# Two heads blocks on one core: where phi's VectorE part stands in the queue, one early transfer, one staging buffer

## The chip, the cores and the metric

The kernel runs on one core of one Trainium2 chip. The metric is the device time of one execution in microseconds (us). A core has five engines that matter here: TensorE (PE in the profile, with its weight loads shown as PEld), VectorE (DVE), ScalarE (ACT), GpSimd (POOL) and SyncE (SP, which issues most of the DMAs). Each engine takes its own instructions strictly in the order in which the program gives them to it, and engines wait for each other through semaphores.

## The reference

Two independent attention blocks run on inputs of 2048 tokens by 640 features, with 32 heads of 20 features, and their outputs are put side by side.

```
# A: attention over a sliding window of 256 keys
q, k, v = split(x @ wqkv)
scores  = q k^T * 20**-0.5, kept where 0 <= query - key < 256
o       = softmax(scores) @ v
a       = o @ wo

# B: linear attention, no softmax
phi(t)  = where(t > 0, t + 1, exp(t)) + 1e-6
kv, z   = sum_s phi(k) v^T, sum_s phi(k)
o       = (phi(q) @ kv) / (phi(q) @ z + 1e-6)
b       = o @ wo

out     = concatenate([a, b], axis=-1)        # bfloat16, 2048 x 1280
```

## The kernel before

All tokens are worked on in four blocks s = 0 to 3 of 512. The program is written out by hand in the order in which each engine is to take it; no scheduler moves anything.

**The score loop.** A's attention is cut into 90 score tiles (`units`, from `tiles_of`). For one tile `scores` lets TensorE write four heads' scores into `S_ps`, a tile of four PSUM banks of which there is one, lets ScalarE take the exponential of all of it into `p` (L582), and lets GpSimd zero what lies outside the window (`affine_select`, L596). Two tiles later (`LAG = 2`) `values` multiplies `p` with the values into `O_ps` (L618), one PSUM bank, of which there is one as well. When a group of heads is done, VectorE takes the reciprocal (`recA`, L640) and writes the normalised rows into `otokA` (L641). The next group's first matmul into `O_ps` has to wait for that.

**The filler.** Between two tiles, `take(credit)` draws matmuls from `fill`, a chain of Python generators with all other work: the projections of q, k and v of A (`a_qk`, `a_v`), the keys and values of B (`b_kv`), phi(q) of B (`b_q`), the denominators (`b_den`), the product of kv and wo (`b_merge`), and the output projections (`a_out`, `b_out`). A credit in matmul columns spreads it evenly over the 90 tiles. Each projection chain accumulates five matmuls into one `dense` PSUM bank (`bank`, `chain`, L201). There are three such banks, and the pool hands out the bank that was given back first in program order. Most banks are emptied by one VectorE copy (`evac`, L192).

**phi.** Where a bank holds B's q or k, `phi` empties it: ScalarE writes exp into a tile `e` (L210), VectorE clamps `e` in place (L214), and a second VectorE instruction (L217) reads the bank and `e` and writes phi. The two VectorE instructions are put off: they go into the list `later`, and `flush` issues them. In the kernel before, `flush` runs behind the next VectorE or ScalarE copy of another bank (`evac`) or behind the next exp (`phi`). For q, the put-off part also issues the DMA transpose `tok<-phi` on SP's queue (L498).

**Loads.** `spread(gen, loads, step)` issues x of a block as four DMA transposes on SP's queue (L689), one at every `step`-th matmul of `gen`. `("B", NS + 1)` stands for x of B's block 1, loaded a second time for `q[1]`, the second phi(q); it runs along with `q[0]`. On the same queue stand the transposes `oT<-otokA` (L652), `tok<-phi` (L498) and `wB<-wB` (L453, five for the merged weights).

**The tail.** After the last tile `a_out_last` projects A's last block, one row of 128 tokens at a time, through a staging buffer `osb` of a pool entry with two buffers, which the earlier output projections also use; their results leave by DMAs from GpSimd's queue (L384), the last ones from SP's (L673). `otokA` is another entry of that pool, also with two buffers.

Of the kernel before, what the change touches and what calls it, by code (L numbers as in the profile page):

```python
# [9 lines left out]
P = 128  # L10
# [3 lines left out]
BF16 = mybir.dt.bfloat16  # L14
# [7 lines left out]
TPS = SB // P  # L22
# [32 lines left out]
def kernel(  # L55
# [11 lines left out]
    _, S, D = A_x.shape  # L67
    KT = D // P
    NS = S // SB
# [7 lines left out]
    def pool(name, bufs, space=None):  # L77
        if space is None:
            return ctx.enter_context(tc.tile_pool(name=name, bufs=bufs))
        return ctx.enter_context(tc.tile_pool(name=name, bufs=bufs, space=space))  # L80
# [12 lines left out]
    op = pool("o", 2)  # L93
# [79 lines left out]


    later = []

    def flush():

        while later:
            later.pop(0)()  # L180

    both = []

    def evac(dst, src, to=None):

        if to is None and both:
            both.append(to)
            to = "AD"[len(both) % 2]
        if to == "A":
            nc.scalar.activation(out=dst, in_=src, func=ACT.Copy)  # L190
        else:
            nc.vector.tensor_copy(out=dst, in_=src)  # L192
        flush()

    def bank():
        return dps.tile([P, SB], F32, name="dense")

    def chain(dst, lhs, rhs, n):

        for kt in range(KT):  # L200
            nc.tensor.matmul(  # L201
                dst, lhsT=lhs(kt), rhs=rhs(kt), start=(kt == 0), stop=(kt == KT - 1)
            )
            if kt < KT - 1:
                yield n

    def phi(dst, src, view=lambda t: t[:], then=None):

        e = ep.tile([P, SB], BF16, name="e")
        nc.scalar.activation(out=view(e), in_=src, func=ACT.Exp)  # L210
        flush()

        def rest():
            nc.vector.tensor_scalar(  # L214
                out=e[:], in0=e[:], scalar1=1e-6, scalar2=1.0 + 1e-6, op0=ALU.add, op1=ALU.min
            )
            nc.vector.scalar_tensor_tensor(  # L217
                out=dst, in0=src, scalar=0.0, in1=view(e), op0=ALU.max, op1=ALU.add
            )
            if then is not None:  # L220
                then()

        later.append(rest)

    class End(int):
        pass
# [9 lines left out]
    def even(a, na, b, nb, lead=False):  # L236


        def one(g):
            for c in g:  # L240
                yield c
                if isinstance(c, End):
                    break

        done = 0
        for i in range(na):
            while lead and done < nb and done * na <= i * nb:
                done += 1
                yield from one(b)
            yield from one(a)  # L250
            while not lead and done * na < (i + 1) * nb:
                done += 1
                yield from one(b)
        yield from a
# [52 lines left out]
    def a_qk(s, between=()):  # L307
        yield from a_rows("q", s)
        for g in between:
            yield from g  # L310
        yield from drip(a_rows("k", s), ("q", s), 10, 4)
# [31 lines left out]
    def a_v(s):  # L343
        v_tok[s] = v_bufs[s % 3]
        yield from v_proj("A", xA[s], v_tok[s])
# [214 lines left out]
    def key(s, rel):  # L560
        return 4 * s + rel

    def scores(s, parts):
        S_ps = sps.tile([P, 4, SB], F32, name="S_ps")
        p_all = pp.tile([P, 4 * SB + 2], BF16, name="p")
        p = p_all[:, 0 : 4 * SB].rearrange("p (j q) -> p j q", j=4)
        nc.scalar.activation(out=p_all[0:1, 4 * SB : 4 * SB + 1], in_=ident[0:1, 0:1], func=ACT.Copy)  # L567
        for g, rel, blk, qs in parts:
            kb = key(s, rel)
            kt = k_pad[kb // TPS]  # L570
            ko = (kb % TPS) * P
            q0, n = qs[0][0] * P, len(qs) * P
            for j in range(4):
                nc.tensor.matmul(  # L574
                    S_ps[:, j, blk * P : blk * P + n],
                    lhsT=kt[32 * j : 32 * j + DH, g, ko : ko + P],
                    rhs=q_pad[s][32 * j : 32 * j + DH, g, q0 : q0 + n],
                    start=True,
                    stop=True,
                    tile_position=(32 * j, 0),  # L580
                )
        nc.scalar.activation(out=p, in_=S_ps[:], func=ACT.Exp, scale=scale)  # L582
        runs = []
        for _, _, blk, qs in sorted(parts, key=lambda x: x[2]):
            for i, (_, kind) in enumerate(qs):
                if kind == "F":
                    continue
                b = blk + i
                if runs and runs[-1][0] == kind and runs[-1][2] == b and b < runs[-1][1] + 2:
                    runs[-1][2] = b + 1  # L590
                else:
                    runs.append([kind, b, b + 1])
        for kind, b0, b1 in sorted(runs, key=lambda r: r[2] - r[1]):
            v = p[:, :, b0 * P : b1 * P].rearrange("p j (b q) -> p j b q", q=P)
            sgn = 1 if kind == "D" else -1
            nc.gpsimd.affine_select(  # L596
                out=v,
                in_=v,
                pattern=[[0, 4], [0, b1 - b0], [sgn, P]],
                compare_op=ALU.is_ge,  # L600
                fill=0.0,
                base=0 if kind == "D" else -1,
                channel_multiplier=-sgn,
            )
        return p
# [51 lines left out]
        yield from wo_proj(wo_sb["A"], 0, oT_A[s], s, 0)  # L657

    def a_out_last(s):
        osb = op.tile([P, TPS, D], BF16, name="osb")  # L660
        for tb in range(TPS):
            for lo, hi, to in ((0, SB, "A"), (SB, D, "D")):
                ps = bank()
                for _ in chain(
                    ps[:, 0 : hi - lo],
                    lambda kt: oT_A[s][:, kt, tb * P : (tb + 1) * P],
                    lambda kt: wo_sb["A"][:, kt, lo:hi],
                    hi - lo,
                ):
                    pass  # L670
                evac(osb[:, tb, lo:hi], ps[:, 0 : hi - lo], to)
            r0 = s * SB + tb * P
            nc.sync.dma_start(out=out2[r0 : r0 + P, 0:D], in_=osb[:, tb, :])  # L673
# [6 lines left out]
    def spread(gen, loads, step):  # L680

        parts = []
        for n, s in loads:
            def part(tb, n=n, s=s):
                x = xA if n == "A" else xB
                if tb == 0:
                    x[s] = xp.tile([P, KT, SB], BF16, name=f"x{n}")
                r0 = s % NS * SB + tb * P
                nc.sync.dma_start_transpose(  # L689
                    out=x[s][:, :, tb * P : (tb + 1) * P], in_=xsrc[n][r0 : r0 + P, :]  # L690
                )
            parts += [(part, tb) for tb in range(TPS)]
        for i, c in enumerate(gen):
            if i % step == 0 and parts:
                fn, tb = parts.pop(0)
                fn(tb)
            yield c
        for fn, tb in parts:
            fn(tb)
# [8 lines left out]
    def seq(*gens):  # L708
        for g in gens:
            yield from g  # L710
# [15 lines left out]
    def late_load(n, w):  # L726

        if w is None:
            load_w(n, B_wqkv, 0, nc.sync)
        elif n == "A":  # L730
            nc.sync.dma_start(out=wo_sb[n][:], in_=w.rearrange("(kt p) n -> p kt n", p=P))
        else:
            g = GH * DH
            whole = w[0 : KT * g, :].rearrange("(c p) n -> p c n", p=g)
            nc.sync.dma_start(out=wo_sb[n][0:g, 0:KT, :], in_=whole)
            nc.sync.dma_start(out=wo_sb[n][0 : D - KT * g, KT, :], in_=w[KT * g : D, :])
# [8 lines left out]
    def k_reads(s, gen):  # L745
        return drip(gen, ("k", s), 8, 5)

    early = seq(a_qk(3), k_reads(3, a_v(3)))
    q = [b_q(s) for s in range(NS)]
# [7 lines left out]
        spread(a_qk(2), [("B", NS)], 10),  # L757
        k_reads(2, a_v(2)),
        b_kv(3),
        spread(even(q[0], KT, early, 3), [("B", NS + 1)], 4),  # L760
        spread(
            seq(banks(q[1], 2), b_den(0), even(q[1], KT - 2, early, 3)), [("B", NS + 2)], 10
        ),
# [26 lines left out]
    credit = 0.0  # L790
    for i, (okey, first, last, parts) in enumerate(units):
        p = scores(okey[0], parts)
        if i in late_loads:
            late_load(*late_loads[i])
        pend.append((okey, first, last, parts, p))
        if len(pend) > LAG:
            values(*pend.popleft())
            credit += rate
        else:
            credit += rate + NO_VALUES  # L800
        credit -= take(credit)
# [4 lines left out]
    for _ in fill:  # L806
        pass
    a_out_last(NS - 1)

# [28 lines left out]
```

## Time and profile before

| | |
|---|---|
| three runs | 279.88, 281.84 (median), 284.75 us |
| profiled execution: its time, its span | 280.25 us, 278.5 us |
| granted TensorE clock in it | 1.000 |
| PE busy | 266.9 us, 96% |
| ACT busy | 201.8 us, 72% |
| DVE busy | 172.7 us, 62% |
| POOL busy | 163.1 us, 59% |

The span runs from the first to the last instruction of the program; the execution's own time is 1.75 us longer than the span. A row of the timeline reads: start in us from the span's start, length in us, engine, source line, operation, output and inputs, shape, number of instructions; in brackets stands how long the engine had been idle before it, and what ended that. Rows of a few instructions are merged into one. Matmuls are pipelined and their ends are modelled, so a short wait of TensorE can be hidden in a row that looks busy; the start of what follows tells it.

### The profile page before, as it was taken

Reading aid. Unit: us, or ns where it says so; the run is one execution under the profiler, and the core shown is the slowest. Engines: PE = TensorE matmul, PEld = TensorE weight load, DVE = VectorE, ACT = ScalarE, POOL = GpSimd, SP = SyncE. Lnnn points to the kernel's source line nnn. Section 1 sums busy time; section 2 is a strip of 40 time slices with the busy share of each in tenths; the row PEclk is TensorE's granted clock in tenths of the full one; section 3 lists DMA queues with packets and bytes.
Section 4 is the critical chain, followed back from the end, with each engine's and each line's share of the span. In section 5 each row is a group of like instructions: output and inputs, shape, how many; then the busy total and the mean of one; then the engine's idle time right before and its main releaser. Section 6 shows DMA issues by size and latency. Waiting matters only on the chain.

```text
span 278.5 us, 8218 instructions
## 1 busy us (share of the span) xinstructions
PE 266.9 (96%) x3474; PEld 155.3 (56%) x3516; DVE 172.7 (62%) x336; ACT 201.8 (72%) x231; POOL 163.1 (59%) x204
## 2 busy tenths in 40 slices
PE   7999999999999999999999899999999999999995
PEld 7744465665665654565664354465644564456542
DVE  0656665657757555554566576987688767866821
ACT  1200039989989887889989899778889889998432
POOL 5000017667656667776669956676687778777710
PEclk9999999999999999999999999999999999999999
DMA  7997596949532994541016624599979744940886
GB/s 248 305 308 215 157 233 164 175 89 201 158 74 47 138 126 113 142 120 34 2 26 120 106 50 101 133 163 192 173 121 151 111 134 126 116 117 28 167 193 209
DMA packets 81214, 38.88 MB, mean 140 GB/s; under 512 B 63897, under 2 KB 80281, under 8 KB 81177
## 3 DMA queue, kind: packets, MB, share of 16 engines
q1 hardware_dynamic: 78857, 32.45, 57.7%
q0 software_dynamic: 1008, 4.59, 5.0%
q10 hardware_dynamic: 1312, 1.31, 1.4%
q8 instruction: 27, 0.44, 0.7%
q14 instruction: 10, 0.08, 0.2%
HBM read 12.45 MB, written 10.49 MB: 82 GB/s over the span
## 4 chain that ended last, share of the span: by engine, by line
PE 82%; ACT 7%; DVE 3%; issue 3%; DMA 2%; POOL 1%; DVEq 0%; POOLq 0%; SPq 0%; ACTq 0%
PE dense L201 52%; PE O_ps L618 14%; PE S_ps L574 10%; ACT p L582 6%; PE dense L415 2%; PE dense L150 2%; DMA xA<-vB 1%; DMA xB<-in_B_x_dram 1%; POOL p L596 1%; PE dense L464 1%; DVE otokA L641 1%; ACT e L210 1%; PE dense L134 1%; DVE tok L534 1%; DVE st L192 0%
## 5 line engine op out<-in xcount | busy, mean ns | idle before, releaser
L596 POOL TENSOR_SCALAR_AFFINE_SELECT p<-p 128x512 bf16<-128x512 bf16 (+1 forms) x180 | 150.9, 839 | 100.7 <-ACT p L582 93.6
L582 ACT ACTIVATE p<-S_ps 128x2048 bf16<-128x2048 f32 x90 | 168.7, 1875 | 39.5 <-PE S_ps L574 39.0
L618 PEld LDWEIGHTS <-p 128*128 128x128 bf16 x1440 | 42.3, 96 | 20.2 <-issue 16.9
L618 PE MATMUL O_ps<-vA,p 128*128 128x21 bf16 x1440 | 50.9, 173 | 1.1 <-DVE otokA L641 0.6
L201 PE MATMUL dense<-wB,xB 128*128 128x320 bf16 (+2 forms) x310 | 48.1, 296 | 1.0 <-DVE vB L192 0.3
L201 PE MATMUL dense<-xA,wA 128*128 128x512 bf16 x191 | 45.3, 379 | 0.6
L192 DVE CAST st<-dense 128x512 bf16<-128x512 f32 x40 | 27.5, 690 | 22.5 <-PE dense L201 19.5
L574 PE MATMUL S_ps<-qpad,kpad 20*128 20x256 bf16 (+2 forms) x736 | 35.9, 269 | 0.9 <-ACT p L582 0.4
L192 DVE CAST osb<-dense 128x512 bf16<-128x512 f32 (+1 forms) x35 | 22.5, 642 | 20.7 <-PE dense L201 19.2
L201 PEld LDWEIGHTS <-xA 128*128 128x128 bf16 x320 | 26.5, 97 | 15.1 <-DMA xA<-vB 1.6
L201 PEld LDWEIGHTS <-xB 128*128 128x128 bf16 x320 | 26.0, 97 | 13.3 <-issue 1.3
L574 PEld LDWEIGHTS <-kpad 20*128 20x128 bf16 x736 | 12.7, 92 | 30.5 <-issue 29.0
L201 PEld LDWEIGHTS <-wA 128*128 128x128 bf16 x200 | 18.5, 97 | 19.9
L217 DVE SCALAR_TENSOR_TENSOR phi<-dense,e 128x512 bf16<-128x512 f32 x40 | 27.7, 692 | 1.4
L567 ACT ACTIVATE p<-ident 1x1 bf16<-1x1 bf16 x90 | 16.9, 188 | 15.4 <-DVE st L192 15.4
L201 PE MATMUL dense<-wB,xA 128*128 128x512 bf16 (+1 forms) x155 | 24.5, 296 | 1.0 <-DMA xA<-vB 0.6
L201 PE MATMUL dense<-xB,wB 128*128 128x512 bf16 x89 | 24.2, 378 | 1.3 <-DMA xB<-in_B_x_dram 0.8
L210 ACT ACTIVATE e<-dense 128x512 bf16<-128x512 f32 x40 | 23.6, 593 | 1.3 <-PE dense L201 0.9
L192 DVE CAST vB<-dense 128x320 bf16<-128x320 f32 x32 | 15.3, 489 | 14.7 <-PE dense L201 14.2
L201 PE MATMUL dense<-woA,oT 128*128 128x128 bf16 (+1 forms) x153 | 23.4, 295 | 0.8 <-DVE osb L192 0.5
L201 PE MATMUL dense<-wA,xA 128*128 128x320 bf16 x160 | 23.9, 299 | 0.1
L192 DVE CAST vA<-dense 128x320 bf16<-128x320 f32 x32 | 15.8, 492 | 9.4 <-PE dense L201 9.3
(41 smaller groups left out, 150.4 us busy)
## 6 DMA issues: line engine op xcount, KB each, us to landing
out_dram<-osb POOLq DMA_DIRECT2D x7, 640.0 KB, 4.3
qpad<-q_scr SPq DMA_DIRECT2D x16, 160.0 KB
kpad<-k_scr SPq DMA_DIRECT2D x16, 160.0 KB
wA<-in_A_wqkv_dram SPq DMA_DIRECT2D x3, 800.0 KB
wB<-in_B_wqkv_dram SPq DMA_DIRECT2D x3, 800.0 KB
q_scr<-st SPq DMA_DIRECT2D x3, 640.0 KB
k_scr<-st SPq DMA_DIRECT2D x3, 640.0 KB
woA<-in_A_wo_dram SPq DMA_DIRECT2D x1, 800.0 KB
```

Source lines behind the costliest of these rows:

```text
L134: nc.tensor.transpose(ps[:, c * P : (c + 1) * P], tok[:, tb, c * P : (c + 1) * P], ident[:])
L150: nc.tensor.matmul(ps[:, 0:P], lhsT=ident[:], rhs=ident[:], start=True, stop=True)
L192: nc.vector.tensor_copy(out=dst, in_=src)
L201: nc.tensor.matmul(dst, lhsT=lhs(kt), rhs=rhs(kt), start=(kt == 0), stop=(kt == KT - 1))
L210: nc.scalar.activation(out=view(e), in_=src, func=ACT.Exp)
L217: nc.vector.scalar_tensor_tensor(out=dst, in0=src, scalar=0.0, in1=view(e), op0=ALU.max, op1=ALU.add)
L415: nc.tensor.matmul(pv[:, i, :, :], lhsT=pk[:, tb, c * P : (c + 1) * P], rhs=vB[:, tb, GH * c : GH * c + NHC, :], start=(tb == 0), stop=(tb ...
L567: nc.scalar.activation(out=p_all[0:1, 4 * SB : 4 * SB + 1], in_=ident[0:1, 0:1], func=ACT.Copy)
L574: nc.tensor.matmul(S_ps[:, j, blk * P : blk * P + n], lhsT=kt[32 * j : 32 * j + DH, g, ko : ko + P], rhs=q_pad[s][32 * j : 32 * j + DH, g, ...
L582: nc.scalar.activation(out=p, in_=S_ps[:], func=ACT.Exp, scale=scale)
L596: nc.gpsimd.affine_select(out=v, in_=v, pattern=[[0, 4], [0, b1 - b0], [sgn, P]], compare_op=ALU.is_ge, fill=0.0, base=0 if kind == "D" el ...
L618: nc.tensor.matmul(O_ps[:, slot, j, :], lhsT=p[:, j, b * P : (b + 1) * P], rhs=v_tok[kb // TPS][:, kb % TPS, 4 * gg + j, :], start=(first ...
```

## The change

There are three edits.

1. The put-off VectorE part of phi carries the number of banks begun so far. `evac` and `phi` no longer issue it. It is issued right behind the matmuls, the exponential and the masks of the next score tile (`flush()` after `scores`), or, where no tile comes first, before the third bank after it is begun (`flush(begun[0] - 2)` in `bank`). `b_kv` and `b_den` still call `flush()` themselves.
2. `spread` of x for `q[1]` has step 1 instead of 4.
3. `a_out_last` takes its staging buffer from the entry `otokA` instead of `osb`.

```diff
     later = []
-
-    def flush():
-
-        while later:
-            later.pop(0)()
+    begun = [0]
+
+    def flush(before=None):
+
+        while later and (before is None or later[0][0] <= before):
+            later.pop(0)[1]()
@@ evac
             nc.vector.tensor_copy(out=dst, in_=src)
-        flush()
 
     def bank():
+        flush(begun[0] - 2)
+        begun[0] += 1
         return dps.tile([P, SB], F32, name="dense")
@@ phi
         nc.scalar.activation(out=view(e), in_=src, func=ACT.Exp)
-        flush()
...
-        later.append(rest)
+        later.append((begun[0], rest))
@@ a_out_last
-        osb = op.tile([P, TPS, D], BF16, name="osb")
+        osb = op.tile([P, TPS, D], BF16, name="otokA")
@@ fill
-        spread(even(q[0], KT, early, 3), [("B", NS + 1)], 4),
+        spread(even(q[0], KT, early, 3), [("B", NS + 1)], 1),
@@ the loop over units
         p = scores(okey[0], parts)
+        flush()
```

TensorE, ScalarE and GpSimd get the same instructions in the same order as before. On VectorE, 23 of phi's 40 pairs move forward (22 of them ahead of one bank copy, 11 ahead of a `recA`/`otokA` pair), two move behind one bank copy, and 15 stay where they were. On SP, the second and third quarter of x for `q[1]` come to stand ahead of four `oT<-otokA` transposes, the fourth ahead of the first `tok<-phi`, and the five `wB<-wB` transposes ahead of the third `tok<-phi`. No instruction is added or removed but waits.

## The prediction

> **What bounds the kernel now.** I read the page's busy times first, then the waits of TensorE, then the timeline of ScalarE, and then the places where the last two meet.
>
> ```profile
> span 278.5 us, 8218 instructions
> PE 266.9 (96%) x3474; PEld 155.3 (56%) x3516; DVE 172.7 (62%) x336; ACT 201.8 (72%) x231; POOL 163.1 (59%) x204
> ```
>
> TensorE is idle for 278.5 - 266.9 = 11.6 us, part of it at the start and the end. That is a first limit: nothing here removes matmuls. The second limit is the score loop:
>
> ```profile
> 176.99 0.40 PE L574 MATMUL S_ps<-qpad,kpad 20*128 20x128 bf16 x8
> 207.18 1.88 ACT L582 ACTIVATE p<-S_ps 128x2048 bf16<-128x2048 f32 x1 [0.41 <-PE S_ps L574]
> 209.55 1.88 ACT L582 ACTIVATE p<-S_ps 128x2048 bf16<-128x2048 f32 x1
> ```
>
> There is one `S_ps`, so the next score matmuls start when the exponential has read it, and the next exponential when they end: 1.88 + 0.40 and some 0.09 of signals make 2.37 us, which is the distance from 207.18 to 209.55. No tile can be faster. 0.41 us is ScalarE's ordinary idle time before an exponential, and a phi exp of 0.59 us just about fills it. Time is lost where TensorE comes late to the score matmuls; there ScalarE's idle time is longer than 0.41. So an edit gains only what it takes from those tiles. TensorE's waits that the edits could touch are few:
>
> ```profile
> PE dense L201 <- DMA xB<-in_B_x_dram: 0.8, 1, 0.8
> PE O_ps L618 <- DVE otokA L641: 0.6, 1, 0.6
> PE dense L201 <- DVE osb L192: 0.5, 1, 0.5
> PE dense L201 <- DVE vB L192: 0.3, 1, 0.3
> ```
>
> **Part 1: phi's VectorE pair.** VectorE has the same work; what counts is who queues behind whom. The clearest place is the tile at 92 us:
>
> ```profile
> 91.86 0.59 ACT L210 ACTIVATE e<-dense 128x512 bf16<-128x512 f32 x1
> 92.35 0.57 PE L618 MATMUL O_ps<-vA,p 128*128 128x21 bf16 x16
> 92.95 0.26 DVE L640 RECIPROCAL recA<-O_ps 128x16 f32<-128x16 f32 x1 [1.76 <-PE O_ps L618]
> 93.24 0.49 DVE L641 TENSOR_TENSOR otokA<-O_ps,recA 128x320 bf16<-128x320 f32 x1
> 93.65 0.48 DVE L192 CAST vB<-dense 128x320 bf16<-128x320 f32 x1
> 94.05 0.28 DVE L214 TENSOR_SCALAR e<-e 128x512 bf16<-128x512 bf16 x1
> 94.37 0.69 DVE L217 SCALAR_TENSOR_TENSOR phi<-dense,e 128x512 bf16<-128x512 f32 x1
> 94.19 0.84 PE L201 MATMUL dense<-wB,xB 128*128 128x320 bf16 x5 [0.31 <-DVE vB L192]
> 95.41 1.88 ACT L582 ACTIVATE p<-S_ps 128x2048 bf16<-128x2048 f32 x1 [0.98 <-PE S_ps L574]
> ```
>
> VectorE stands idle for 1.76 us although exp is done at 91.86 + 0.59 = 92.45, because the pair is queued behind a copy that comes 1.2 us later. Phi's bank is held until 95.06, the chain at 94.19 gets the copy's bank instead, and the exponential comes 0.98 - 0.41 = 0.57 late. In the changed order the pair runs at 92.5 and ends at 92.5 + 0.28 + 0.69 = 93.5; its bank is then the first one back, before TensorE asks for it at 94.19 - 0.31 = 93.88. Gain: 0.31 by TensorE's wait, 0.57 by ScalarE's; the rest of that lateness may be the tile's own filler, so I take **0.45**.
>
> ```profile
> 221.27 0.59 PE L201 MATMUL dense<-woA,oT 128*128 128x512 bf16 x2 [0.48 <-DVE osb L192]
> 222.24 1.88 ACT L582 ACTIVATE p<-S_ps 128x2048 bf16<-128x2048 f32 x1 [0.93 <-PE S_ps L574]
> ```
>
> The same pattern at 221 us, with a copy into `osb`: 0.48 by TensorE, 0.93 - 0.41 = 0.52 by ScalarE. I take **0.5**.
>
> ```profile
> 174.33 0.69 DVE L217 SCALAR_TENSOR_TENSOR phi<-dense,e 128x512 bf16<-128x512 f32 x1
> 175.53 1.62 DVE L534 TENSOR_TENSOR tok<-tok,rden 128x640 bf16<-128x640 bf16 x1
> 177.99 0.55 PE L618 MATMUL O_ps<-vA,p 128*128 128x21 bf16 x16 [0.60 <-DVE otokA L641]
> 180.45 1.88 ACT L582 ACTIVATE p<-S_ps 128x2048 bf16<-128x2048 f32 x1 [1.05 <-PE S_ps L574]
> ```
>
> Here two quotient instructions (1.62 us) push `otokA` back. The pair before them moves ahead of one copy, but the other copy in front of the quotients still waits for its own chain, and the quotients stay. Bounds 0 and 0.60; I take **0.3**, half, as the pair is one of three things in front.
>
> ```profile
> 58.57 1.88 ACT L582 ACTIVATE p<-S_ps 128x2048 bf16<-128x2048 f32 x1 [0.88 <-PE S_ps L574]
> ```
>
> One more tile is late by 0.88 - 0.41 = 0.47, at the end of a stretch of phi banks, with no wait shown, so the filler's own length has a share. Bounds 0 and 0.47; I take **0.2**, somewhat under the half. The other moved pairs stand in tiles that run at 2.37 already: nothing.
>
> The pair now also delays what it overtakes. At 92 us `recA` and `otokA` would end at 93.5 + 0.26 + 0.49 = 94.25 instead of 93.73; the next values may start one period after 92.35, at 94.72. So 0.47 us is left, and the delay costs nothing, at 11 such places, as long as the clamp (L214) stays short. It is not always:
>
> ```profile
> L214 DVE TENSOR_SCALAR e<-e x40: 282/332/801, 43.4 to 246.3; 128x512 bf16<-128x512 bf16 x40
> 84.89 1.84 POOL L596 TENSOR_SCALAR_AFFINE_SELECT p<-p 128x512 bf16<-128x512 bf16 x2 [0.54 <-ACT p L582]
> 85.34 0.37 DVE L214 TENSOR_SCALAR e<-e 128x512 bf16<-128x512 bf16 x1 [0.30 <-ACT e L210]
> 216.57 0.80 DVE L214 TENSOR_SCALAR e<-e 128x512 bf16<-128x512 bf16 x1
> ```
>
> At 94.05 the clamp took its least, 0.28. At 85.34 it began, as the moved ones will, the moment exp ended, while GpSimd was masking, and took 0.37; the longest, at 216.57, took 0.80. I take 0.37, the row with the same phase, since exp, masks and score matmuls keep their distances: 0.09 of the 0.47 is used.
>
> **Part 2: x for the second phi(q).**
>
> ```profile
> 145.76 5.16 SPq L652 DMA_TRANSPOSE oT<-otokA  x4
> 150.97 2.60 SPq L689 DMA_TRANSPOSE xB<-in_B_x_dram  x2
> 153.67 1.64 SPq L498 DMA_TRANSPOSE tok<-phi  x1
> 155.35 1.28 SPq L689 DMA_TRANSPOSE xB<-in_B_x_dram  x1
> 155.35 3.08 DMA xB<-in_B_x_dram
> 158.56 1.46 PE L201 MATMUL dense<-xB,wB 128*128 128x512 bf16 x6 [0.79 <-DMA xB<-in_B_x_dram]
> 158.66 0.59 ACT L210 ACTIVATE e<-dense 128x512 bf16<-128x512 f32 x1
> 159.84 0.60 ACT L210 ACTIVATE e<-dense 128x512 bf16<-128x512 f32 x1 [0.59 <-PE dense L201]
> 160.43 1.85 ACT L582 ACTIVATE p<-S_ps 128x2048 bf16<-128x2048 f32 x1
> ```
>
> The last quarter is issued at 155.35, behind a `tok` transpose that waits for VectorE, and lands 3.08 us later (the chain of waits has this row); TensorE has waited 0.79 us. In the new order quarters two and three (1.3 us each) go out in SP's pause before 145.76, and the fourth right after the four `oT`, at 150.97: it lands at about 154.1, over 3 us before TensorE wants it. What is late next is ScalarE: two exps stand between the exponentials. The second could begin when the first ends, 159.25, instead of 159.84, so the exponential at 160.43 comes 0.59 earlier, not 0.79. I take **0.6**, between 0.5 and 0.8. The five `wB` transposes and the third `tok` change places; SP issues the same number in the same stretch, and the first reader of `tok` is the quotient at 175.53 above, some ten us after that stretch; the merge comes behind it: nothing.
>
> **Part 3: the staging buffer.**
>
> ```profile
> 270.89 0.60 ACT L190 ACTIVATE osb<-dense 128x512 bf16<-128x512 f32 x1 [0.53 <-PE dense L201]
> ```
>
> The first write into the buffer waited 0.53 us for TensorE, not for an output DMA. The other buffer was last read by the third block's transposes, long landed. **0**; were a wait there, the 0.53 us of idle time would cover it.
>
> **Sum.** 0.45 + 0.5 + 0.3 + 0.2 + 0.6 = 2.05 us. From the profiled execution's own 280.25 that gives **278.2 us**. The median of the three runs shown, 281.84, is 1.6 above that execution, the lowest, 279.88, is 0.4 below it.
>
> **The rivals.** (a) *The stalls only move on.* TensorE's waits on VectorE end in tiles whose next wait, the exponential, is already close: the waits list gives only 0.8 us to the one transfer and 1.4 to VectorE. If VectorE's gains turn into waits for `S_ps` and the transfer alone counts, the time is 280.25 - 0.6 = 279.6. For it: most tiles run at 2.37 with no margin. Against: the tiles at 95, 180 and 222 are 0.5 to 0.6 late, and that is above the floor.
>
> (b) *Banks come back earlier in every phi stretch, and more late tiles catch up.* Besides the named tiles others may be late by 0.1 us or so, hidden in rows that look busy (an estimate); with 23 moved pairs at 0.1 each, 2.3 us more: 275.9. Against it: no wait in the list names VectorE there.
>
> (c) *Slower: the clamp is held by GpSimd's masks.* It now starts inside the masks everywhere. If it waits out one whole mask instruction (1.84 / 2 = 0.92 us) before its own 0.28, the pair at 92 us ends at 92.5 + 0.92 + 0.28 + 0.69 = 94.39, `otokA` at 95.14, and the next values, due at 94.72, are 0.42 late. It decides from a clamp of 0.28 + 0.47 = 0.75 us on. At 11 places that is 4.6 us; VectorE's gains are gone and the transfer's 0.6 stays: 280.25 + 4.6 - 0.6 = 284.3. For it: the 0.80 at 216.57, where clamp and mask begin together. Against: 0.37 at 85.34.
>
> The Trainium skill speaks for (c): "SBUF — State Buffer", section "SBUF: two separate sides", says that VectorE in a two-port mode and GpSimd take turns on a shared pair of ports, the one that starts first holding it for its whole instruction. By that rule a clamp can be held up to the 0.92 us used in (c), and the sum is (c)'s 284.3 at worst; the trace agrees with the direction (0.28 to 0.80), and 0.37 in the new phase speaks against the size.
>
> (d) *The change doesn't do what it says*: the fourth quarter still stands behind the `oT` transposes, which wait for `otokA`. If `otokA` came 3 us later, the 0.6 would be gone: 278.8, within the forecast's own range.
>
> **How the numbers follow.** Forecast (with d) 0.55, own range 277.3 to 279.0 (each term at its bounds: 0.31 + 0.48 + 0 + 0 + 0.5 = 1.3 and 0.57 + 0.52 + 0.6 + 0.47 + 0.8 = 3.0); (a) 0.2; (b) 0.13; (c) 0.12. The range takes in (b), (a) and half of (c), and the runs' spread to the upper side: 275.3 to 282.8. Over 2%, about what a measurement of this kernel can tell from no change, is 5.6 us. None of the cases reaches it by its centre: faster needs (b) at its full and more, 0.09; slower needs (c) at more than 11 places, 0.08; within, 0.83.
>
> **What would show it.** Right: VectorE's copies gone from TensorE's waits; exponentials near 95 and 222 at 2.4 to 2.5 us from the one before; the `xB` wait gone and two exps in a row in that tile; clamps mostly 0.3 to 0.4. Wrong: clamps of 0.8 and more in the moved places with TensorE waiting for `otokA`; a new wait of TensorE for `oT` or `wB`; or the late tiles still late with another releaser.

## The result and the profile after

The changed kernel takes 278.31 us (median; the lowest run 277.95), the kernel before, over its runs on the same chip, 281.81 us (279.88 to 284.75). The ratio is 0.989, with a 95% interval of 0.985 to 0.993: about 1% faster. One of the eight runs of the changed kernel took 326.16 us at a granted clock of 0.756, and such runs are left out of all ratios here. The profiled execution of after takes 278.2 us, that of before 280.25.

The first view to compare is the span with the row of the score exponential in the list of the tile `p`. It gives the number of exponentials, their shortest, median and longest time in ns, and the start of the first and of the last. The first fence is after, the second before.

```profile
span 276.5 us, 8270 instructions
L584 ACT ACTIVATE p<-S_ps x90: 1850/1877/1878, 38.5 to 256.4; 128x2048 bf16<-128x2048 f32 x90
```

```profile
L582 ACT ACTIVATE p<-S_ps x90: 1849/1877/1877, 38.6 to 258.6; 128x2048 bf16<-128x2048 f32 x90
```

From the first to the last exponential passed 258.6 - 38.6 = 220.0 us before and 217.9 after. From the last exponential to the end of the span it was 278.5 - 258.6 = 19.9 before and 20.1 after. So all of the gain between these two executions, 2.1 us, is in the score loop. The medians differ by more, 3.5 us here and 2.35 us when the changed kernel was run again; what goes beyond 2.1 is not shown to come from the change. (The second decimals used below for single tiles come from the starts in the timeline.)

The tile at 92 us, in the timeline of after, all engines, only the rows that the prediction showed of before:

```profile
92.17 0.37 DVE L216 TENSOR_SCALAR e<-e 128x512 bf16<-128x512 bf16 x1 [1.29 <-ACT e L213]
...
92.45 1.79 PE L203 MATMUL dense<-wB,xB 128*128 128x320 bf16 x12
...
92.64 0.69 DVE L219 SCALAR_TENSOR_TENSOR phi<-dense,e 128x512 bf16<-128x512 f32 x1
...
93.53 0.49 DVE L643 TENSOR_TENSOR otokA<-O_ps,recA 128x320 bf16<-128x320 f32 x1
...
94.62 1.88 ACT L584 ACTIVATE p<-S_ps 128x2048 bf16<-128x2048 f32 x1 [0.51 <-PE S_ps L576]
```

The pair (92.17 and 92.64) now runs right behind exp and ahead of `otokA`. Twelve matmuls go through without a wait where TensorE had waited 0.31 for the copy. ScalarE's idle time before the exponential fell from 0.98 to 0.51. The other tiles that the prediction named, in the same timeline:

```profile
58.32 1.88 ACT L584 ACTIVATE p<-S_ps 128x2048 bf16<-128x2048 f32 x1 [0.68 <-PE S_ps L576]
...
174.09 0.90 DVE L536 TENSOR_TENSOR tok<-tok,rden 128x640 bf16<-128x640 bf16 x1
175.20 0.49 DVE L643 TENSOR_TENSOR otokA<-O_ps,recA 128x320 bf16<-128x320 f32 x1
...
178.82 1.88 ACT L584 ACTIVATE p<-S_ps 128x2048 bf16<-128x2048 f32 x1 [0.41 <-PE S_ps L576]
...
220.09 1.88 ACT L584 ACTIVATE p<-S_ps 128x2048 bf16<-128x2048 f32 x1 [0.50 <-PE S_ps L576]
```

The idle time at 58 us fell from 0.88 to 0.68, at 222 us from 0.93 to 0.50, and at 180 us from 1.05 to 0.41, which is the floor. At 174.09 one quotient instruction stands ahead of `otokA` as before (`x1` in both rows), but it takes 0.90 us where it had taken 1.62.

x for the second phi(q), on SP's queue and ScalarE:

```profile
140.04 4.46 SPq L691 DMA_TRANSPOSE xB<-in_B_x_dram  x3
...
149.87 1.28 SPq L691 DMA_TRANSPOSE xB<-in_B_x_dram  x1
...
155.79 1.88 ACT L584 ACTIVATE p<-S_ps 128x2048 bf16<-128x2048 f32 x1 [0.53 <-PE S_ps L576]
157.56 1.08 ACT L213 ACTIVATE e<-dense 128x512 bf16<-128x512 f32 x2
...
158.61 1.85 ACT L584 ACTIVATE p<-S_ps 128x2048 bf16<-128x2048 f32 x1
```

The last quarter is issued at 149.87 instead of 155.35, TensorE no longer waits for it, and the two exps run in one row of 1.08. The exponential follows the one before it by 158.61 - 155.79 = 2.82 us; before it was 3.54.

Two tiles got slower that had run at the floor before. All engines, the rows around them:

```profile
159.20 0.53 DVE L216 TENSOR_SCALAR e<-e 128x512 bf16<-128x512 bf16 x1
...
160.65 0.49 DVE L643 TENSOR_TENSOR otokA<-O_ps,recA 128x320 bf16<-128x320 f32 x1
...
160.96 1.88 ACT L584 ACTIVATE p<-S_ps 128x2048 bf16<-128x2048 f32 x1
...
161.29 0.55 PE L620 MATMUL O_ps<-vA,p 128*128 128x21 bf16 x16 [0.38 <-POOL p L598]
...
163.75 1.88 ACT L584 ACTIVATE p<-S_ps 128x2048 bf16<-128x2048 f32 x1
...
165.69 1.84 POOL L598 TENSOR_SCALAR_AFFINE_SELECT p<-p 128x512 bf16<-128x512 bf16 x2 [0.84 <-ACT p L584]
...
166.60 1.08 DVE L216 TENSOR_SCALAR e<-e 128x512 bf16<-128x512 bf16 x1 [1.02 <-ACT e L213]
...
168.61 0.49 DVE L643 TENSOR_TENSOR otokA<-O_ps,recA 128x320 bf16<-128x320 f32 x1
...
168.90 1.88 ACT L584 ACTIVATE p<-S_ps 128x2048 bf16<-128x2048 f32 x1 [0.40 <-PE S_ps L576]
...
169.24 0.55 PE L620 MATMUL O_ps<-vA,p 128*128 128x21 bf16 x16 [0.39 <-POOL p L598]
...
171.69 1.88 ACT L584 ACTIVATE p<-S_ps 128x2048 bf16<-128x2048 f32 x1 [0.35 <-PE S_ps L576]
```

The distances are 163.75 - 160.96 = 2.79 and 171.69 - 168.90 = 2.79, against 2.38 before at both: 0.83 us lost together. The brackets of the two value matmuls name GpSimd's `p`. But that work was ready earlier: the masks at 165.69 end at 167.53, 1.7 us ahead of 169.24. `otokA` ends at 168.61 + 0.49 = 169.10, and the values start 0.14 later; in the other place 161.14 and 0.15 later. That is also the distance in the row of before where the profile names `otokA` itself (177.84 to 177.99). So VectorE was last, and of the clamps in front of it one took 1.08 us, the other 0.53.

There are also four tiles with a gain at which the prediction put nothing: 2.54 to 2.37 us at 131 us, 2.54 to 2.38 at 141, 2.68 to 2.60 at 214, and 2.44 to 2.37 near 76. The first of them, before and then after:

```profile
129.31 1.88 ACT L582 ACTIVATE p<-S_ps 128x2048 bf16<-128x2048 f32 x1
...
130.90 0.28 DVE L214 TENSOR_SCALAR e<-e 128x512 bf16<-128x512 bf16 x1
...
131.85 1.88 ACT L582 ACTIVATE p<-S_ps 128x2048 bf16<-128x2048 f32 x1
```

```profile
128.52 1.88 ACT L584 ACTIVATE p<-S_ps 128x2048 bf16<-128x2048 f32 x1
128.54 0.37 DVE L216 TENSOR_SCALAR e<-e 128x512 bf16<-128x512 bf16 x1 [1.50 <-ACT e L213]
...
130.89 1.88 ACT L584 ACTIVATE p<-S_ps 128x2048 bf16<-128x2048 f32 x1
```

It is the pattern of 92 us in small: the clamp came 1.59 us after the exponential began, and now comes at its start. No wait was shown there; only the distance of 2.54 gave it away.

The account of the loop by distances between exponentials, in us: -0.19 (58 us), -0.07 (one tile near 76), -0.47 (95), -0.16 (131), -0.17 (141), -0.72 (160), -0.64 (180), -0.08 (214), -0.43 (222), together -2.93; +0.41 (165) and +0.42 (172), together +0.83; sum -2.10. All other tiles are as before, to 0.03.

### The profile page after: what moved, and what is told of

The parts are those of the page before. It is cut to its first block, busy times and chain, and to the rows that moved or that the text cites. A ratio compares the mean times of both kernels' runs of the same rounds, so it can differ in the third digit from the quotient of the medians.

```text
span 276.5 us, 8270 instructions
## 1 busy us (share of the span) xinstructions
PE 268.1 (97%) x3516; PEld 155.5 (56%) x3516; DVE 172.8 (62%) x336; ACT 201.8 (73%) x231; POOL 164.1 (59%) x204
## 4 chain that ended last, share of the span: by engine, by line
PE 84%; ACT 6%; POOL 3%; issue 3%; DMA 2%; DVE 0%; POOLq 0%; ACTq 0%
PE dense L203 55%; PE O_ps L620 13%; PE S_ps L576 10%; ACT p L584 5%; POOL p L598 2%; PE dense L417 2%; DMA xA<-vB 2%; PE dense L150 2%; PE dense L466 1%; ACT e L213 1%; POOL wB L164 1%; PE dense L514 1%; PE dense L134 0%; POOL zk L164 0%; ACT otokA L191 0%
## 5 line engine op out<-in xcount | busy, mean ns | idle before, releaser
L620 PEld LDWEIGHTS <-p 128*128 128x128 bf16 x1440 | 42.4, 96 | 20.1 <-issue 17.1
L203 PE MATMUL dense<-xA,wA 128*128 128x512 bf16 x200 | 46.5, 379 | 0.0
L193 DVE CAST osb<-dense 128x512 bf16<-128x512 f32 x31 | 21.2, 687 | 14.5 <-PE dense L203 14.2
L203 PEld LDWEIGHTS <-wA 128*128 128x128 bf16 x200 | 18.5, 97 | 19.9
L216 DVE TENSOR_SCALAR e<-e 128x512 bf16<-128x512 bf16 x40 | 16.7, 417 | 20.3 <-ACT e L213 20.2
L203 PE MATMUL dense<-wB,xA 128*128 128x512 bf16 (+1 forms) x160 | 25.3, 299 | 1.1 <-DMA xA<-vB 1.1
L203 PE MATMUL dense<-xB,wB 128*128 128x512 bf16 x100 | 26.1, 378 | 0.0
L203 PE MATMUL dense<-woA,oT 128*128 128x512 bf16 (+1 forms) x160 | 24.1, 298 | 0.0
```

The costliest lines, as they stand in the source:

```text
L203: nc.tensor.matmul(dst, lhsT=lhs(kt), rhs=rhs(kt), start=(kt == 0), stop=(kt == KT - 1))
L216: nc.vector.tensor_scalar(out=e[:], in0=e[:], scalar1=1e-6, scalar2=1.0 + 1e-6, op0=ALU.add, op1=ALU.min)
L620: nc.tensor.matmul(O_ps[:, slot, j, :], lhsT=p[:, j, b * P : (b + 1) * P], rhs=v_tok[kb // TPS][:, kb % TPS, 4 * gg + j, :], start=(first ...
```

## The experiments

Ratios are to the kernel before on the same chip, with 95% intervals. The whole times of one kernel spread by up to 6 us (the kernel before, over 35 runs, from 279.14 to 285.04), while the changed kernel, profiled twice, has the same loop both times (217.9 us) and differs behind the last exponential, as shown further down. So single stages are read from the loop's row and from distances between exponentials. In these two executions they repeat to 0.01 us. The exception seen is a tile that waits for a transfer: with the same order for x, the tile at 160 us took 3.54 us in the kernel before and 3.79 with the staging buffer alone.

**x alone.** The kernel before with step 1 for x.

```diff
-        spread(even(q[0], KT, early, 3), [("B", NS + 1)], 4),
+        spread(even(q[0], KT, early, 3), [("B", NS + 1)], 1),
```

> The kernel before with only x of B's second phi(q) issued at step 1. Theory (each edit pays in its own tiles): the tile at 160 us gets its second exp at once and is 0.6 to 0.8 us shorter, the other late tiles (95, 180, 222 us) stay as they were; time 279.5 against 280.25 for the profiled execution of before, ratio 0.997. Rival (the transfer was hidden anyway, or the stall only moves to the next wait): the tiles after 160 us give it back, ratio 1.000. A second point: before's runs spread over 279.9 to 284.8 us, those of the changed kernel mostly over 278.0 to 278.4. If a transfer that lands late by a varying time makes that spread, it is gone here; if not, it stays.

Measured: 0.9975 [0.9947, 1.0004], median 279.8 us. The tile in question; the loop takes 219.2 us, 0.7 less than before:

```profile
156.78 1.88 ACT L582 ACTIVATE p<-S_ps 128x2048 bf16<-128x2048 f32 x1 [0.53 <-PE S_ps L574]
158.56 1.08 ACT L210 ACTIVATE e<-dense 128x512 bf16<-128x512 f32 x2
159.60 1.85 ACT L582 ACTIVATE p<-S_ps 128x2048 bf16<-128x2048 f32 x1
```

The distance is 2.82, exactly that of after; the gain of 0.72 (0.97 against the 3.79 just named) belongs to this edit alone. The other late tiles stay as they were before (2.95, 3.01, 2.89), and the two new stalls are not there.

**The phi edit alone.** The kernel before with edit 1 only.

> The kernel before with only the edit on phi's VectorE part. Theory: tiles at 95, 180 and 222 us shorter by 0.4 to 0.65 each, those at 58, 131 and 141 us by 0.15 to 0.2, none of the stall on x gone (tile at 160 us still 3.5 us); time about 278.9, ratio 0.995. The two tiles behind 160 us that became 0.42 us longer in the changed kernel become so here as well, if the order on VectorE makes them; if the earlier x makes them (two exps close together), at most one of them does. Rival on the spread of the runs: if the late transfer makes it, it stays here (2 to 4 us).

Measured: 0.9969 [0.9934, 1.0004], median 279.71 us.

```profile
L584 ACT ACTIVATE p<-S_ps x90: 1849/1877/1877, 38.6 to 257.4; 128x2048 bf16<-128x2048 f32 x90
```

```profile
153.96 2.39 SPq L691 DMA_TRANSPOSE xB<-in_B_x_dram  x1
...
158.21 1.46 PE L203 MATMUL dense<-xB,wB 128*128 128x512 bf16 x6 [1.42 <-DMA xB<-in_B_x_dram]
...
170.29 0.55 PE L620 MATMUL O_ps<-vA,p 128*128 128x21 bf16 x16 [0.38 <-POOL p L598]
```

The late tiles of VectorE's kind have all of after's gain (2.65, 2.48, 2.37 and 2.46 in place of 2.84, 2.95, 3.01 and 2.89). But the wait for x grew from 0.79 to 1.42 (one execution each, at the tile that varies), and the loop is only 1.2 us shorter, 218.8. The stall at 172 us is there (170.29 waits 0.38), so the phi edit alone makes it; the one at 165 us is not (2.37), so that one needs both edits, which bring the two exps of 157.56 together. The parts therefore don't add up: 0.72 and 1.16 alone, 2.10 together. Together, the 0.63 of longer waiting for x falls away and the stall of 0.41 is added.

**The staging buffer alone.**

```diff
-        osb = op.tile([P, TPS, D], BF16, name="osb")
+        osb = op.tile([P, TPS, D], BF16, name="otokA")
```

> The kernel before with only the last projection's staging buffer taken from the other pool entry. Theory (the first write never waited for a transfer): no change, ratio 1.000 within the interval, and the first ScalarE copy of the last projection still waits about 0.5 us for TensorE. Rival (in slower executions the output transfer of GpSimd's queue lands late and holds the buffer): lower time by 1 us or more, and a smaller spread.

Measured: 0.9991 [0.9957, 1.0025], median 280.46 us. No tile changes but the one that waits for x (3.54 to 3.79 us), which this edit does not touch, and the first copy into the buffer still waits for TensorE (0.73 us of idle time ahead of it). It has no effect that can be seen.

**`otokA` first at the two new stalls.** The changed kernel, in which, before two tiles, the newest put-off pair is kept back until `recA` and `otokA` have been issued.

```diff
         p = scores(okey[0], parts)
+        kept = [later.pop()] if i in (49, 52) and later else []
         flush()
...
             values(*pend.popleft())
+            later[:0] = kept
+            flush()
```

> The changed kernel, with the newest phi pair put behind recA/otokA again at two tiles only, those after which the score period grew by 0.42 us. Theory (the pair in front of otokA holds up the next values there): both periods fall back to 2.38 to 2.45 us, 0.8 us in all; time 277.5 against 278.3, ratio 0.9845 to before. Rival 1 (GpSimd's masks come late there, as the releaser's name says): periods unchanged, time 278.3. Rival 2 (the pair that now waits gives its bank back late, and a chain waits instead): the periods fall, and others near by grow as much.

Measured: 0.9917 [0.9882, 0.9952], median 277.34 us.

```profile
159.71 0.49 DVE L643 TENSOR_TENSOR otokA<-O_ps,recA 128x320 bf16<-128x320 f32 x1
...
161.19 1.88 ACT L584 ACTIVATE p<-S_ps 128x2048 bf16<-128x2048 f32 x1
...
163.56 1.88 ACT L584 ACTIVATE p<-S_ps 128x2048 bf16<-128x2048 f32 x1
...
168.72 1.88 ACT L584 ACTIVATE p<-S_ps 128x2048 bf16<-128x2048 f32 x1 [0.40 <-PE S_ps L576]
...
171.10 1.88 ACT L584 ACTIVATE p<-S_ps 128x2048 bf16<-128x2048 f32 x1
```

```profile
L584 ACT ACTIVATE p<-S_ps x90: 1849/1877/1877, 38.8 to 255.8; 128x2048 bf16<-128x2048 f32 x90
```

Both tiles are back at 2.37 and 2.38, and nothing else grew: 217.0 us from first to last exponential against 217.9. Only VectorE's order differs here. That shows the stalls to be VectorE's, not GpSimd's as the brackets of after said.

**Masks left out.** The changed kernel without the masks of `p`, which takes GpSimd's work beside the clamps away.

```diff
-        for kind, b0, b1 in sorted(runs, key=lambda r: r[2] - r[1]):
+        for kind, b0, b1 in []:
```

> The changed kernel with GpSimd's masks of p left out (A attends to keys outside its window), so GpSimd is idle in the score loop. Theory (the clamp is held by a mask that is under way): the clamp's median falls from 0.37 to its least, 0.28 us, and its longest, 1.08 us at 166.6 us, is gone, except where GpSimd masks B's sums (148 to 156 us); the score period at 171.7 us falls from 2.79 towards 2.38. The period at 163.8 us, where two pairs stand ahead of recA, falls by a few tenths at most. Rival (the clamp is long because ScalarE still writes e, or because of VectorE's own queue): median 0.37 and the long ones stay.

Measured in a single run: 276.07 us. The kernel then gives weight to keys outside the window. The row of the clamp in the list of the tile `e`, after and then without masks, there with the row of the quotients from the list of `tok`:

```profile
L216 DVE TENSOR_SCALAR e<-e x40: 283/370/1082, 43.4 to 244.2; 128x512 bf16<-128x512 bf16 x40
```

```profile
L216 DVE TENSOR_SCALAR e<-e x40: 282/294/295, 42.8 to 242.8; 128x512 bf16<-128x512 bf16 x40
L536 DVE TENSOR_TENSOR tok<-tok,rden x8: 812/815/825, 172.5 to 236.8; 128x640 bf16<-128x640 bf16 x8
```

All 40 clamps now take their least time, and the two tiles run at 2.39 and 2.37. I had expected the one at 165 us to fall by a few tenths at most; it fell by 0.40, all of its loss but 0.02. So its clamp of 0.53 and the one ahead of it were held as well. The quotients were held too: the eight into `tok` now take at most 0.825 us, where the longest took 1.62 in the kernel before.

**Earlier quotients, twice.** The time behind the last exponential differs with the landings of the transposes `xA<-vB` of the last quotients. That is seen in the chain that ended last, of the kernel with x alone (start, length, step):

```profile
257.31 5.80 DMA xA<-vB
263.33 4.73 DMA xA<-vB
```

Two landings end there one after the other, and 21.6 us pass from the last exponential to the end. In the profiled execution of after there is one in that chain (5.64 us), and 20.1 us pass. The same kernel executed once more, the run further down, has two (5.47 and 5.26), and 21.7 us pass.

Two versions, both on the kernel with `otokA` first twice, issue the quotients earlier: first by a denser step, then ahead of all remaining output projections.

```diff
-        with_quotients(b_out(2), (3,), 2, 4),
+        with_quotients(b_out(2), (3,), 1, 2),
```

> The kernel with otokA first at two tiles, and the last four quotients issued at every second matmul of B's third output projection instead of every fourth, from the first on. The end of the runs differs: from the last exponential's start to the end it is 19.8 to 20.1 us in some and 21.6 us in others. Theory (the four transposes behind these quotients land 5 to 6 us after their issue, by a varying amount, and TensorE waits for them): they go out 1 to 1.5 us earlier, the wait for xA<-vB falls from 0.8 to 1.3 us to near 0, time 276.3 to 276.8, ratio 0.988, and the runs spread less. Rival (the last transposes of A's rows, oT, are as late): the time stays within 0.3 us of 277.3.

Measured: 0.9948 [0.9923, 0.9972], median 279.47 us; 2.1 above the kernel it was made from, though on another chip. The ratios, 0.9948 against 0.9917, put it 0.9 us above. The wait for `xA` is gone, but TensorE has others in the tail, two of them for `oT` (0.40 and 0.86 us), and one tile of the loop, near 200 us, is 0.47 us longer, where TensorE's weight load waits 0.39 us for keys (`kpad<-k_scr`). Why `oT` lands later here stays open; a collision with an output DMA of GpSimd's queue is only argued.

The runs spread from 279.18 to 279.82, 12 of them, while the kernel before spreads from 279.26 to 284.21 beside it. That would fit the landing of `xA` as the maker of the spread. x's late quarter does not make it: with x alone, early, the runs still go from 278.54 to 283.99.

```diff
-        outs,
         b_den(3),
-        with_quotients(b_out(2), (3,), 2, 4),
+        with_quotients(outs, (3,), 2, 4),
+        b_out(2),
```

> The kernel with otokA first at two tiles, and B's last denominators and quotients moved ahead of the rest of A's third output projection, some 8 us earlier. Theory (the landing of the last transposes makes both the wait in the tail and the spread of the runs): no wait for xA<-vB at all, spread of most runs under 1 us, time 276.0 to 276.6. Rival 1 (oT is as late): 277.0 or more, with TensorE waiting for oT instead. Rival 2 (the spread is not from there): the runs still reach 2 us and more above the lowest.

Measured: 0.9999 [0.9972, 1.0027], median 280.77 us. The gain is gone altogether: in the score loop TensorE now waits 1.67 us for phi before the denominators, the first quotient 0.73 us for its own transposes, and two tiles grow to 4.68 and 3.39 us. TensorE does not wait for `xA` in the profiled execution here either, yet the runs go from 279.31 to 281.78; "under 1 us" was wrong. Seven of the twelve had a granted clock of 0.994, and they are at 280.72 and above; of the five at 1.000, four are at 279.31 to 279.78. In the kernel before, on the same chip, the four runs above 283 us are those at 0.994 or less as well. So part of the spread goes with the granted clock, and how much of the rest the landing of `xA` makes is not shown.

**The changed kernel and `otokA` first, once more on one chip.**

> The changed kernel itself, beside the next one on one chip. Theory: ratio to before 0.989 to 0.993, and both tiles with otokA behind a phi pair at 2.79 us again.

> The changed kernel with the newest phi pair behind recA/otokA at two tiles, beside the changed kernel on one chip. Theory: 0.8 us faster than the changed kernel in its lower runs, ratio to before lower by 0.003. Rival (the tail waits for the same transfers anyway and takes it back): within 0.3 us of it.

Measured: the changed kernel 0.9928 [0.9902, 0.9954], median 278.32, lowest 277.44 us; `otokA` first twice 0.9896 [0.9863, 0.9929], median 277.82, lowest 276.6. The exponentials, the changed kernel and then `otokA` first:

```profile
L584 ACT ACTIVATE p<-S_ps x90: 1849/1877/1879, 37.9 to 255.8; 128x2048 bf16<-128x2048 f32 x90
```

```profile
L584 ACT ACTIVATE p<-S_ps x90: 1849/1877/1877, 38.6 to 255.6; 128x2048 bf16<-128x2048 f32 x90
```

217.9 against 217.0: the loop is shorter by the same amount as in the first pair. In whole time the two intervals overlap, so that 0.8 us of 278 is shown by the loop's row twice, and by the times only as a tendency. It is the fastest version here that computes the same.

## Why the prediction was right, and where it was not

The time came out as forecast, and by the main mechanism: late tiles got their bank or their `otokA` sooner, and x its ScalarE. But that the sum of 2.05 meets the 2.10 measured in the loop is luck: the forecast terms gave 2.45, tiles without a forecast another 0.48, and an unforecast cost took 0.83 back. That the profiled execution took the very 278.2 is luck as well: the second profiled execution of the same kernel took 279.21, with the same loop and 1.6 us more behind it.

- *92 us, 0.45 forecast:* 0.47. *221 us, 0.5:* 0.43. *58 us, 0.2:* 0.19. The step (the pair behind the copy keeps phi's bank) holds; with the phi edit alone the same distances appear.
- *180 us, 0.3:* 0.64. The term was mis-sized, and even its upper bound of 0.60 was just too low. The step that failed is "the quotients stay", on a row that was misread: the 1.62 us at 175.53 are one quotient (`x1`), not two, and it did not stay. Since the moved pair no longer stands between the two copies, the quotient starts 0.02 us behind its tile's exponential instead of 0.47, and it takes 0.90 instead of 1.62; `otokA` is done 1.16 us earlier in the turn. Why it is shorter is shown below.
- *x, 0.6:* 0.72, within its bounds, and shown alone (the size varies with the landing in the kernel before, as said). What was late next was ScalarE, as forecast: two exps in a row take 1.08, a little less than the 1.18 that two single ones of 0.59 make.
- *Staging buffer, 0:* nothing to be seen, alone and in the sum.
- *"The other moved pairs stand in tiles that run at 2.37 already: nothing":* wrong in four tiles, 0.48 us together. Rival (b) was true there, and only there, not at 23 pairs. I had read lateness from brackets, and these tiles show none that stands out; distances between exponentials would have shown 2.54 at two of them.
- *"The delay costs nothing at 11 places":* wrong at two, 0.83 us. The clamp was taken at 0.37, "the row with the same phase", which is its median after (370 ns), but at these two places the phase is another, and the clamp takes 1.08 and 0.53. This is rival (c), true at 2 of its 11 places: `otokA` first removes it by taking the pair out of the way, and leaving the masks out removes it by making the clamps short.

What holds the clamp is the mask that it begins in. The price in (c), 1.84 / 2 = 0.92 us a mask, rests on a merged row; in narrow windows of GpSimd's timeline the two masks stand apart. First, from after, the mask around the clamp of 92.17 (0.37 us), the mask around that of 166.60 (1.08) and the mask around the quotient of 174.09 (0.90); then, from before, the mask around the quotient of 175.53 (1.62):

```profile
91.71 0.68 POOL L598 TENSOR_SCALAR_AFFINE_SELECT p<-p 128x512 bf16<-128x512 bf16 x1 [0.54 <-ACT p L584]
...
166.44 1.10 POOL L598 TENSOR_SCALAR_AFFINE_SELECT p<-p 128x1024 bf16<-128x1024 bf16 x1
...
173.64 0.68 POOL L598 TENSOR_SCALAR_AFFINE_SELECT p<-p 128x512 bf16<-128x512 bf16 x1 [0.95 <-ACT p L584]
```

```profile
175.38 1.10 POOL L596 TENSOR_SCALAR_AFFINE_SELECT p<-p 128x1024 bf16<-128x1024 bf16 x1
```

The mask of 91.71 ends at 92.39 and its clamp at 92.54; the mask of 166.44 ends at 167.54 and its clamp at 167.68. Both clamps end 0.15 us behind their mask, and in the whole trace of after 35 of the 40 do, to within 0.01. The two quotients end 0.67 us behind their masks. So 0.37 is no smaller price but the same one: that clamp begins 0.46 us into a mask of 0.68, the one of 1.08 begins 0.16 us into a mask of 1.10, and each waits out what is left. The clamp of 159.20, at the other new stall, begins 0.72 us into a mask of 1.10 and takes 0.53. The quotient got shorter by the same rule: before, it began 0.15 us into a long mask, after, 0.45 us into a short one. The Trainium skill's rule that VectorE and GpSimd take a shared pair of ports in turn, each for a whole instruction ("SBUF — State Buffer", section "SBUF: two separate sides"), fits that. The trace agrees with it in size too, at 0.37 as at 1.08, so the prediction's 0.37 did not speak against it.

Against rival (a): TensorE's waits on VectorE copies did not turn into other waits in their tiles. Against (d): the last quarter of x was issued 5.9 us ahead of the tile's preceding exponential (149.87 and 155.79), where before it had been 1.5 (155.35 and 156.89).

## What to carry to other kernels

Where a loop has a floor per turn, list the distances between the turns' starts, before and after: that finds hidden lateness that no bracket shows, and the turns that lose what others gain. A long distance alone is no gain yet: the tile at 154 us had 2.82 and kept it. When work is moved ahead of something with little slack, look at each place by itself, and price it by what the moved instruction will begin in: here by what is left of GpSimd's mask and 0.15 us more. Two of eleven places cost 0.83 us, and putting `otokA` first there brought it back. Read the count and the shape of a merged row before a length is divided by it. Where a wait is named after an engine that had long been done, look for the work that ended just ahead of the waiting instruction, and change the order of that work alone to prove it.

## What the runs showed of the hardware that was not expected

- A clamp of 128x512 bf16 on VectorE takes 0.28 to 0.295 us alone (all 40 without masks). One that begins in a GpSimd mask ends 0.15 us behind that mask, in 35 of 40 cases in the changed kernel, so that it takes anything up to 1.08 us. The quotients, 128x640 bf16, at most 0.825 us alone, took up to 1.62 in the same way.
- The transposes `xA<-vB` at the end take 4.7 to 5.8 us each in the rows shown, and whether one or two of them stand in the chain that ended last differs between two executions of the changed kernel (20.1 and 21.7 us behind the last exponential). Of the two kernels whose profiled execution is without that wait one spread by 0.6 us and the other by 2.5; what makes the landing vary was not found.
- Runs of the kernel with the quotients ahead of all output projections at a granted clock of 0.994 took 280.72 to 281.78 us, those at 1.000 mostly 279.31 to 279.78.
